# Running AV, MoE and w2*wout as pairs of 64-row tiles on TensorE, with scores in a ring of two

## The chip, the cores and the metric

The kernel runs on one core of one Trainium2 chip. Its engines work side by side, each through its own instruction stream in order, and meet at semaphores: TensorE (PE) multiplies matrices and writes to PSUM, ScalarE (ACT) and VectorE (DVE) read PSUM, GpSimd (POOL) casts inputs in SBUF, and SyncE (SP) issues nearly all transfers. PSUM has eight banks of 512 fp32 columns for each of 128 partitions. A matmul here is a weight load (the stationary operand, up to 128 rows by 128 columns) and a stream of up to 512 columns.

The metric is the device time in microseconds. Three timed runs of the kernel before gave 384.52, 386.2 and 386.59 us; their median is 386.2.

## The reference: what is computed

Attention with queries averaged in pairs, for batch 8, 8 heads, 1152 keys and head dimension 64, followed by an expert layer:

```python
q_pool = q.reshape(B, H, S // 2, 2, D).mean(axis=3)
scores = 1 / sqrt(D) * matmul(q_pool, k.transpose(0, 1, 3, 2))
attn   = softmax(scores)                       # over 1152 keys
x      = matmul(attn, v)   -> (4608 tokens, 512)
h1, h2 = x @ w1, x @ w2                        # 512 -> 1024
out    = maximum(h1, h2) @ w_out               # 1024 -> 512
```

The kernel uses max(h1, h2) = relu(x(w1 - w2)) + x w2. So it forms wd = w1 - w2 and w21 = w2*w_out once, computes g = relu(x wd), and then out = x w21 + g w_out.

## The kernel before, in words

**Stages.** The unit of attention is a pair of heads: 8 batches x 4 = 32 pairs. Q, K and V of a pair are loaded, cast to bf16 (queries are summed two by two) and transposed, the first pairs by TensorE, later ones by transposing transfers. The kinds of TensorE work are:

- *scores* (L429). The 9 key tiles x 576 queries of all pairs form one line, cut into 324 groups of 512 columns. Head dimension 64 fills half the array's rows, so the two heads of a pair use rows 0-63 and 64-127 as two tiles and write two banks. A group occupies one of three PSUM slots `sps` of two banks each.
- *exp* (L436). ScalarE reads one slot, 128x1024, and writes the exponentials as bf16 into `et`.
- *AV* (kind "a", L378). For one head: 5 chunks of queries, each a sum over 9 key tiles of a matmul with 128 rows and 65 columns (64 of V and one of ones, which gives the softmax's denominator). All chunks of a head go to one bank. VectorE takes the reciprocal (L388) and scales (L390).
- *x* (L489): after 4 pairs a batch's x is transposed; batches 0 and 7 by TensorE.
- *w* (L531, L547): w2 is transposed, then multiplied by w_out: 4 jobs of 8 matmuls.
- *h* (L582): for a block of up to 512 tokens, 8 jobs of 4 matmuls; VectorE applies relu into a ring of 1024 tokens (L593).
- *p* (L609): for 128 tokens, a job of 4 + 8 matmuls of 512 columns; the result is copied (L623) and stored (L567).

**How the order is made.** A planner in Python (class `Plan`) simulates the engines with costs and hand-over times (`LAT`), and emits instructions in the order in which it placed them. It also derives the semaphore waits, so on the chip each engine follows this fixed order. A `Job` is a list of units that accumulate into one bank, and an evacuation. Two `lane`s, one for each of the two banks `fb`, hold a job each. In each step (L906 to L937) free lanes are refilled in the order q, k, x, a, w, p, h; then a burst of two or three score groups is emitted if all of it can start now (`burst_now`, `burst_size`), otherwise the unit of highest rank (q, k, x, a, w, p, h) that is ready. Scores are emitted in bursts because the planner charges 0.1 us whenever TensorE goes between "s" (64 rows) and "f" (128 rows).

**The tail.** When all scores are out (`nxt == NGR`), the six banks of `sps` become six more lanes (`more_banks`), and ScalarE takes part in evacuations (L589, L620).

Of the kernel before, what the change touches and what calls it, by code (L numbers as in the profile page):

```python
# [7 lines left out]
P = 128  # L8
# [7 lines left out]
class Plan:  # L16
# [9 lines left out]
    LAT = {"PE": 0.16, "ACT": 0.13, "DVE": 0.1, "POOL": 0.05}  # L26
# [28 lines left out]
    def op(self, eng, fn, r=(), w=(), dma=None, cost=0.1, mode="f", after=(), solo=False):  # L55
        n = len(self.ops)
        assert all(k in self.writer for k in r), r
        deps, raw = self.deps(r, w, after)
        prev = self.last.get(eng)
# [4 lines left out]
        t = self.when(eng, r, w, after)  # L64
        if dma is not None:
# [9 lines left out]
        self.ops.append(dict(eng=eng, fn=fn, deps=deps, raw=raw, dma=dma, w=tuple(w),  # L75
                             seen=seen, end=self.free[eng], solo=solo))
# [7 lines left out]
    def solve(self):  # L84
# [3 lines left out]
        for n, o in enumerate(ops):  # L88
# [3 lines left out]
            for d in sorted(o["deps"], reverse=True):  # L92
                p = ops[d]
                if p["dma"] is None:
                    if p["eng"] == eng and (eng == "PE" or d not in o["raw"]):
# [50 lines left out]
class Job:  # L146


    def __init__(self, kind, units, evac, done=None, nb=None):
        self.kind, self.units, self.evac, self.done = kind, units, evac, done  # L150
        self.nb = nb


def bass_funnel_attn__then__act_maxout2_kernel(
# [12 lines left out]
    SQ = S // 2  # L167
# [16 lines left out]
    NGR = NPAIR * PW // W  # L184

    ctx = ExitStack()
    with ctx:
# [33 lines left out]
        sps = [psum([P, 2, 512], f"sps{g}") for g in range(3)]  # L221
        fb = [psum([P, 512], f"fb{g}") for g in range(2)]
        fb += [sps[g][:, half, :] for g in range(3) for half in range(2)]
# [84 lines left out]
        def unit(r, cost, go, mode="f"):  # L308

            def plan_it(m):  # L310
                op("PE", lambda e: go(e, m), r=r, w=[f"f{m}"], cost=cost, mode=mode)
            return r, plan_it, cost
# [52 lines left out]
        def av_jobs(i):  # L365
# [7 lines left out]
            def chunk(half, sb):  # L373

                def go(e, m):
                    for t in range(NT):
                        a = (half * 2 + es) * PW + t * SQ + sb * P
                        last = e.matmul(  # L378
                            fb[m][:, sb * 66:sb * 66 + 65], et[:, a:a + P],
                            vE[vs][:, t, half, 0:65], start=(t == 0), stop=(t == NT - 1))  # L380
                    return last
                return unit(need, 0.275, go)
# [14 lines left out]
            return [Job("a", [chunk(half, sb) for sb in range(NCH + 1)], norm(half), nb=i)  # L397
# [25 lines left out]
        def scores(g):  # L423
            r = g % 3
# [9 lines left out]
            def exp(a, z, keys):  # L434
# [3 lines left out]
                    r=[f"s{r}"], w=keys + [f"s{r}"], cost=0.24 + (z - a) / 700.0)  # L438
# [103 lines left out]
        def w21_jobs():  # L542
            jobs = []
            for ct in range(NC_):
                def part(ft, ct=ct):
                    def go(e, m):
                        return e.matmul(fb[m][:, :], w2T[:, ct, ft, :], wo[:, ft, :],  # L547
                                        start=(ft == 0), stop=(ft == NF - 1))
                    return unit([f"w2T{ct}", f"wo{ft}"], 0.216, go)
# [4 lines left out]
                jobs.append(Job("w", [part(ft) for ft in range(NF)], evac))  # L554
# [19 lines left out]
        def h_jobs(nb, tail):  # L574
# [4 lines left out]
            for ft in range(NF):  # L579
                def part(ct, ft=ft):  # L580
                    def go(e, m):
                        return e.matmul(fb[m][:, 0:size], wd[:, ct, ft * P:(ft + 1) * P],  # L582
                                        xT[:, ct, n0:n1], start=(ct == 0), stop=(ct == NC_ - 1))
                    return unit([f"wd{ct}"] + xkeys(n0, n1), 0.216 * size / 512, go)

                def evac(m, ft=ft):
                    w = [f"gT.{g}.{ft}" for g in gkeys(n0, n1)] + [f"f{m}"]
                    if tail and ft % 2:
# [7 lines left out]
                jobs.append(Job("h", [part(ct) for ct in range(NC_)], evac, nb=nb))  # L596
            return jobs

        def p_job(lo, tail):
            hi = lo + P  # L600

            def part(j):
                def go(e, m):
                    if j < NC_:
                        lhs, rhs = xT[:, j, lo:hi], w21[:, j, :]
                    else:
                        c = lo % RING
                        lhs, rhs = gT[:, j - NC_, c:c + P], wo[:, j - NC_, :]
                    return e.matmul(fb[m][:, :], lhs, rhs, start=(j == 0), stop=(j == NC_ + NF - 1))  # L609
                if j < NC_:  # L610
                    return unit([f"w21{j}"] + xkeys(lo, hi), 0.216, go)
                return unit([f"wo{j - NC_}", f"gT.{lo % RING // P}.{j - NC_}"], 0.216, go)

            def evac(m):
# [4 lines left out]
                if tail and ocount[0] % 2:  # L619
# [6 lines left out]
            return Job("p", [part(j) for j in range(NC_ + NF)], evac, nb=hi)  # L626
# [3 lines left out]
        lane = {0: None, 1: None}  # L630
# [23 lines left out]
        LAG = 600  # L654
        Q_PE = 5

# [100 lines left out]
        def more_banks():  # L757

            for g in range(3):
                for half in range(2):  # L760
                    m = 2 + 2 * g + half
                    lane[m] = None
                    plan.writer[f"f{m}"] = plan.writer[f"s{g}"]
                    plan.readers[f"f{m}"] = set(plan.readers[f"s{g}"])

        def ready_at(job):
            return plan.when("PE", r=job.units[0][0])

        def burst_size():

            done = [b for b in range(B) if all(av_half.get(b * NHP + j) == 2 for j in range(NHP))]
            return 3 if len(done) * SQ - p_end[0] > LAG else 2

        def more_moe():
            tail = nxt == NGR
            while h_at[0] < len(hblocks):
# [6 lines left out]
                queue["h"].extend(h_jobs(h_at[0], tail))  # L783
                h_at[0] += 1
            while p_at[0] + P <= h_end[0] and f"w21{NC_ - 1}" in plan.writer:
                queue["p"].append(p_job(p_at[0], tail))
                p_at[0] += P

        def refill():
# [3 lines left out]
            for kind in "qkxa":  # L793
                if queue[kind] and (ready_at(queue[kind][0]) <= soon):
                    return queue[kind].pop(0)
            busy = [j.kind for j in lane.values() if j]
            for kind in "wh" if queue["a"] and "p" in busy else "wph":
                if queue[kind] and ready_at(queue[kind][0]) <= soon:
                    return queue[kind].pop(0)
# [6 lines left out]
        def burst_now(size):  # L806

            todo_g = range(nxt, min(nxt + size, NGR))
            if not todo_g:
                return None, 0.0  # L810
            for g in todo_g:
                for p, t, *_ in pieces(g):
                    if p not in q_done or k_hi.get(p, 0) <= t or (
                            p >= 2 and av_half.get(p - 2) != 2):
                        return None, 0.0
            t = now() + 0.1
            stall = 0.0
            for g in todo_g:
                s = plan.when("PE", r=skeys(g), w=[f"s{g % 3}"])
                stall += max(0.0, s - t)  # L820
                t = max(t, s) + PE_S
            return todo_g, stall

        def emit_burst(todo_g):
            nonlocal nxt, entered
            for g in todo_g:
                while entered < pairs_of(g)[-1]:
                    entered += 1
                    enter(entered)
                scores(g)  # L830
                for p in pairs_of(g):
                    if g == after(p) - 1:
                        queue["a"].extend(av_jobs(p))
            nxt += len(todo_g)
            if nxt == NGR:
                more_banks()
            if queue["q"]:
                for kk in (0, 1):
                    if lane[kk] is None and plan.when(
                            "PE", r=queue["q"][0].units[0][0], w=[f"f{kk}"]) <= now() + 0.05:  # L840
                        lane[kk] = queue["q"].pop(0)
                        emit_unit(kk)
                        break

        def emit_unit(kk):
            job = lane[kk]
            plan_it = job.units.pop(0)[1]
            plan_it(kk)
            if job.units:
                return  # L850
            job.evac(kk)
            lane[kk] = None
            if job.kind == "a":
# [52 lines left out]
        while p_end[0] < NTOK:  # L906
            flush()
            for kk in sorted(lane, key=lambda kk: plan.when("PE", w=[f"f{kk}"])):
                if lane[kk] is None:
                    lane[kk] = refill()  # L910
            cand = []
            for kk in lane:
                job = lane[kk]
                if job is not None:
                    t = plan.when("PE", r=job.units[0][0], w=[f"f{kk}"])
                    cand.append((t, -rank[job.kind], len(job.units), kk))
            fresh = [c for c in cand if c[0] <= now() + 0.03]
            ready, stall = burst_now(burst_size())
            if ready and stall <= 0.1:
                emit_burst(ready)  # L920
            elif fresh:
                emit_unit(min(fresh, key=lambda c: c[1:])[3])
            else:
                wait = min([c[0] for c in cand], default=1e9) - now()
                if ready:
                    wait = min(wait, stall)
                size = burst_size()
                while size > 1 and (not ready or stall > 0.05):
                    size -= 1
# [63 lines left out]
```

## Time and profile before

| | |
|---|---|
| median of three timed runs | 386.2 us (384.52 to 386.59) |
| the profiled execution | 382.8 us, its span; the page gives no other time for it |
| PE busy | 363.7 us, 95% of the span |
| ACT busy | 316.9 us, 83% |
| DVE, POOL busy | 140.2 us (37%), 162.0 us (42%) |
| chain that ended last, by engine | PE 85%, DMA 6%, DVE 4%, POOL 2% |
| its largest lines | AV 22%, p 21% + 4%, scores 18%, h 15% + 2% |
| scores on TensorE | from 8.3 to 332.3 us |

How to read it: one execution, all times in us from its start unless marked ns. A row of a group has line, engine, operation, output<-inputs, rows*columns of the weights, shapes and count, then busy time and mean ns of one, then the engine's idle time before it and what ended that. A matmul's duration includes the time until its result is there, so matmuls that follow each other overlap and their starts tell the pace. In a timeline row the first number is the start, the second the time until the last of the merged instructions ended. A row of the chain has the start and the time that it stood in the chain.

### The profile page before, as it was taken

To read this page: it belongs to the slowest core of one execution; us is meant where nothing else is said; L and a number is where in the kernel's file an instruction comes from. 1 tells how busy PE (TensorE), PEld (TensorE's weight loads), DVE (VectorE), ACT (ScalarE), POOL (GpSimd) and SP (SyncE) were. 2 spreads that over 40 slices of the span, in tenths; PEclk is the share of its full clock that TensorE was granted. 3 is DMA by queue.
4 is the path that set the end of the run, shared out by engine and by line. 5 is a ranking of instruction groups with operands and counts; after the bars stand their busy time and mean duration, and the time that the engine had idled before them with its cause. 6 is when DMAs were issued, how large, how long until landed. Compare 5 with 4: busy or idle time off the path is not lost.

```text
span 382.8 us, 11318 instructions
## 1 busy us (share of the span) xinstructions
PE 363.7 (95%) x5010; PEld 210.8 (55%) x5010; DVE 140.2 (37%) x283; ACT 316.9 (83%) x355; POOL 162.0 (42%) x135
## 2 busy tenths in 40 slices
PE   2787999999999999999999999999999999999995
PEld 1365546555555555455556565555455655667642
DVE  2274934442234223422252224422442244237201
ACT  3998989999999999999999999999899999902210
POOL 1955597665554555555453535545545110000000
PEclk9999999999999999999999999999999999999999
DMA  8999999999989998999799999999899460121144
GB/s 248 405 391 399 392 257 312 331 309 312 225 234 295 273 272 174 309 320 275 142 265 289 319 179 212 286 258 315 200 236 267 94 109 14 29 44 42 29 95 98
DMA packets 93521, 88.58 MB, mean 231 GB/s; under 512 B 66080, under 2 KB 66592, under 8 KB 93472
## 3 DMA queue, kind: packets, MB, share of 16 engines
q1 hardware_dynamic: 93472, 87.86, 89.4%
q8 instruction: 39, 0.64, 0.7%
q14 instruction: 10, 0.08, 0.1%
HBM read 62.91 MB, written 9.44 MB: 189 GB/s over the span
## 4 chain that ended last, share of the span: by engine, by line
PE 85%; DMA 6%; DVE 4%; POOL 2%; issue 1%; SPq 1%; POOLq 0%
PE fb L378 22%; PE fb L609 21%; PE sps L429 18%; PE fb L582 15%; PE sps L609 4%; DMA qraw<-in_q_dram 3%; DMA kraw<-in_k_dram 2%; PE sps L582 2%; DVE wd L519 2%; POOL qp L297 1%; PE fb L547 1%; DVE xnat L390 1%; POOL vE L304 1%; PE fb L489 1%; DVE wo L523 1%
## 5 line engine op out<-in xcount | busy, mean ns | idle before, releaser
L436 ACT ACTIVATE et<-sps 128x1024 bf16<-128x1024 f32 (+1 forms) x336 | 307.8, 1005 | 19.0 <-PE sps L429 17.2
L378 PEld LDWEIGHTS fb<-vE,et 128*128 128x128 bf16 x2880 | 93.4, 97 | 20.9 <-issue 10.9
L378 PE MATMUL fb<-vE,et 128*128 128x65 bf16 x2880 | 101.9, 193 | 0.3
L297 POOL TENSOR_TENSOR qp<-qraw 64x576 bf16<-64x576 f32 x62 | 88.6, 1429 | 30.6 <-DMA qpT<-qp 21.3
L429 PE MATMUL sps<-qpT,kT 64*128 64x512 bf16 (+7 forms) x1152 | 96.9, 289 | 3.0 <-ACT et L436 2.1
L304 POOL TENSOR_SCALAR vE<-vraw 128x1152 bf16<-128x1152 f32 x32 | 36.9, 1152 | 103.2 <-PE fb L378 95.8
L429 PEld LDWEIGHTS sps<-qpT,kT 64*128 64x128 bf16 x1152 | 41.8, 95 | 51.3 <-issue 19.6
L582 PE MATMUL fb<-xT,wd 128*128 128x512 bf16 (+3 forms) x276 | 63.1, 360 | 0.7 <-DVE stage L623 0.7
L609 PE MATMUL fb<-wo,stage 128*128 128x512 bf16 x240 | 62.4, 380 | 0.0
L593 DVE TENSOR_SCALAR stage<-fb 128x512 bf16<-128x512 f32 (+3 forms) x64 | 41.9, 657 | 32.3 <-PE fb L582 32.1
L388 DVE RECIPROCAL rc<-fb 128x5 f32<-128x5 f32 x64 | 12.4, 194 | 112.3 <-PE fb L378 112.3
L273 POOL TENSOR_SCALAR kbf<-kraw 128x1152 bf16<-128x1152 f32 x31 | 36.2, 1167 | 14.6 <-DMA kraw<-in_k_dram 12.5
L582 PEld LDWEIGHTS fb<-xT,wd 128*128 128x128 bf16 x276 | 22.8, 98 | 29.4 <-DVE stage L593 6.3
L623 DVE COPY stage<-fb 128x512 f32<-128x512 f32 x29 | 20.0, 690 | 50.2 <-PE fb L609 49.7
L609 PEld LDWEIGHTS fb<-wo,stage 128*128 128x128 bf16 x240 | 21.1, 97 | 23.3 <-issue 3.3
L390 DVE TENSOR_TENSOR xnat<-fb,rc 128x320 bf16<-128x320 f32 x64 | 31.5, 491 | 2.2
L609 PE MATMUL fb<-w,xT 128*128 128x512 bf16 x120 | 32.1, 380 | 0.0
L609 PEld LDWEIGHTS fb<-w,xT 128*128 128x128 bf16 x120 | 10.3, 98 | 11.7 <-issue 2.0
L589 ACT ACTIVATE stage<-sps 128x256 bf16<-128x256 f32 (+1 forms) x7 | 2.3, 338 | 16.4 <-PE sps L582 16.4
L620 ACT COPY stage<-sps 128x512 f32<-128x512 f32 x3 | 1.8, 585 | 13.8 <-PE sps L609 13.8
L609 PE MATMUL sps<-wo,stage 128*128 128x512 bf16 x48 | 11.3, 379 | 0.0
L582 PE MATMUL sps<-xT,wd 128*128 128x256 bf16 (+2 forms) x76 | 10.3, 275 | 0.0
(40 smaller groups left out, 96.4 us busy)
## 6 DMA issues: line engine op xcount, KB each, us to landing
vraw<-in_v_dram SPq DMA_DIRECT2D x32, 576.0 KB, 7.7
kraw<-in_k_dram SPq DMA_DIRECT2D x31, 576.0 KB, 6.6
qraw<-in_q_dram SPq DMA_DIRECT2D x31, 576.0 KB, 5.8
out_dram<-stage SPq DMA_DIRECT2D x72, 128.0 KB, 2.4
xT<-in_moe_w_dram SPq DMA_DIRECT2D x4, 512.0 KB, 11.9
stage<-in_moe_w_out_dram SPq DMA_DIRECT2D x4, 512.0 KB, 14.2
stage<-in_moe_w_dram SPq DMA_DIRECT2D x4, 512.0 KB, 13.2
qraw<-in_q_dram SPq DMA_DIRECT2D x2, 288.0 KB, 4.1
```

The costliest lines, as they stand in the source:

```text
L273: op("POOL", lambda g: g.tensor_scalar(kbf[s][:, :, :, :].rearrange("p t h d -> p h t d"), kraw[r][:, :, :, :], 1.0, 1.0, ALU.mult, ALU.mu ...
L297: op("DVE" if i == 0 else "POOL", lambda g, half=half, a=a: g.tensor_tensor(qp[s][:, :, half, :], a[:, :, 0, :], a[:, :, 1, :], ALU.add), ...
L304: op("POOL", lambda g: g.tensor_scalar(vE[r][:, :, :, 0:D].rearrange("p t h d -> p h t d"), vraw[r][:, :, :, :], 1.0, 1.0, ALU.mult, ALU.m ...
L378: last = e.matmul(fb[m][:, sb * 66:sb * 66 + 65], et[:, a:a + P], vE[vs][:, t, half, 0:65], start=(t == 0), stop=(t == NT - 1))
L388: dve(lambda e: e.reciprocal(rc[half][:, :], a[:, :, 64:65]), [f"f{m}"], [f"rc{half}"], 0.19)
L390: dve(lambda e: e.tensor_tensor(xnat[xs][:, :, c:c + D], a[:, :, 0:D], rc[half][:, :].unsqueeze(2).to_broadcast([P, NCH + 1, D]), ALU.mult ...
L429: last = e.matmul(sps[r][:, h, col:col + hi - lo], kT[i % 3][rows(h), t, :], qpT[i % 3][rows(h), lo:hi], start=True, stop=True)
L436: op("ACT", lambda e: e.activation(et2[:, :, c:c + z - a], sps[r][:, :, a - g * W:z - g * W], EXP, scale=scale), r=[f"s{r}"], w=keys + [f" ...
L582: return e.matmul(fb[m][:, 0:size], wd[:, ct, ft * P:(ft + 1) * P], xT[:, ct, n0:n1], start=(ct == 0), stop=(ct == NC_ - 1))
L593: dve(lambda e: e.tensor_scalar_max(gT[:, ft, g0:g0 + size], fb[m][:, 0:size], 0.0), [f"f{m}"], w, 0.1 + size / 960.0)
L609: return e.matmul(fb[m][:, :], lhs, rhs, start=(j == 0), stop=(j == NC_ + NF - 1))
L623: dve(lambda e: e.tensor_copy(osb[o][:, :], fb[m][:, :]), [f"f{m}"], [f"osb{o}", f"f{m}"], 0.63)
```

## The change

**Pairs.** AV, h, p and w2*wout jobs are marked `split`. Before the last score, two neighbouring jobs of the same kind are taken together as a `Pair`, in a lane of two banks. Each matmul of 128 rows becomes two of 64 rows. In the first half the lower rows work on job one and the upper rows on job two, each into its own job's bank; in the second half the lower rows work on job two and the upper rows on job one. So each job gets both halves of its rows in turn, and the two tiles never write the same bank at the same time. Before the first unit of the second half TensorE waits on its own semaphore until the last matmul of the first half is complete (`gate`); the planner holds that unit back for another 0.2 us (`GATE`), during which it may place other units. When the pair ends, both banks are evacuated one after the other. Only the first matmul of a bank has `start` set. Paired units have mode "s", like the scores.

**Scores.** `sps` becomes a ring of two (`NS = 2`); the banks that this frees give two lanes of two banks. Groups are emitted one at a time, as soon as the slot is free, if the array is in mode "s", or ScalarE would soon run out, or no unit of mode "f" is ready. The bursts go.

**Planner.** The hand-over of ScalarE is now 0.2 us (0.13 before), and an exponential costs 0.08 + columns/612 (0.24 + columns/700 before): 0.917 us for a whole group instead of 0.971. Units of the current mode come first when that mode is "f".

**Tail.** When all scores are out, lanes that are free are split into lanes of one bank (`part_lanes`), and jobs run singly with 128 rows as before.

```diff
-    LAT = {"PE": 0.16, "ACT": 0.13, "DVE": 0.1, "POOL": 0.05}
+    LAT = {"PE": 0.16, "ACT": 0.2, "DVE": 0.1, "POOL": 0.05}
...
+class Pair:
+    def __init__(self, one, two):
+        self.kind, self.jobs = one.kind, (one, two)
+        self.units = []
+        n = len(one.units)
+        for phase in range(2):
+            for k, (u, v) in enumerate(zip(one.units, two.units)):
+                low, high = (u, v) if phase == 0 else (v, u)
+                parts = []
+                for j, (p, q) in enumerate(zip(low.parts, high.parts)):
+                    first = phase == 0 and k == 0 and j == 0
+                    last = phase == 1 and k == n - 1 and j == len(u.parts) - 1
+                    parts.append((p, q, phase, first, last))
+                r = list(dict.fromkeys(list(u.r) + list(v.r)))
+                self.units.append(Unit(r, u.cost * 1.01, "s", parts=parts, gate=phase == 1 and k == 0))
...
-        sps = [psum([P, 2, 512], f"sps{g}") for g in range(3)]
-        fb = [psum([P, 512], f"fb{g}") for g in range(2)]
+        sps = [psum([P, 2, 512], f"sps{g}") for g in range(NS)]
+        S0 = 8 - 2 * NS
+        fb = [psum([P, 512], f"fb{g}") for g in range(S0)]
...
+            def crossed(e):
+                for p, q, phase, first, fin in u.parts:
+                    for half, (at, lhs, rhs, *_), m in ((0, p, ms[phase]), (1, q, ms[1 - phase])):
+                        last = e.matmul(fb[m][:, at:at + rhs.shape[-1]], lhs[rows(half)], rhs[rows(half)],
+                                        start=first, stop=fin)
+                return last
...
-            r = g % 3
+            r = g % NS
...
-                    r=[f"s{r}"], w=keys + [f"s{r}"], cost=0.24 + (z - a) / 700.0)
+                    r=[f"s{r}"], w=keys + [f"s{r}"], cost=0.08 + (z - a) / 612.0)
...
+        def part_lanes():
+            for kk in range(S0 // 2):
+                if lane[kk] is None and len(at_bank[kk]) == 2:
+                    one, two = at_bank[kk]
+                    at_bank[kk] = (one,)
+                    lane[S0 + two] = None
+                    at_bank[S0 + two] = (two,)
...
+        def lane_at(kk):
+            u = lane[kk].units[0]
+            t = plan.when("PE", r=u.r, w=fk(banks_for(kk, lane[kk])))
+            return max(t, plan.ops[gates[kk]]["seen"] + GATE) if u.gate else t
...
+        def take(kind, by):
+            line_up = queue[kind]
+            if not line_up:
+                return None
+            if nxt == NGR or not line_up[0].split:
+                if ready_at(line_up[0]) <= by:
+                    return line_up.pop(0)
+            elif len(line_up) > 1 and line_up[1].split and max(ready_at(j) for j in line_up[:2]) <= by:
+                return Pair(line_up.pop(0), line_up.pop(0))
+            return None
...
-            ready, stall = burst_now(burst_size())
-            if ready and stall <= 0.1:
-                emit_burst(ready)
+            same = [c for c in fresh if lane[c[3]].units[0].mode == plan.mode]
+            ts = score_at()
+            starving = plan.free.get("ACT", 0.0) < now() + 0.6
+            if ts is not None and ts <= now() + 0.03 and (plan.mode != "f" or starving or not same):
+                emit_scores()
             elif fresh:
-                emit_unit(min(fresh, key=lambda c: c[1:])[3])
+                emit_unit(min(same if plan.mode == "f" and same else fresh, key=lambda c: c[1:])[3])
```

More of the change, by code (lines that the diff above doesn't have):

```diff
@@ L373, in chunk @@
             def chunk(half, sb):
[L375 to L382, printed above, removed]
+                parts = []
+                for t in range(NT):
+                    a = (half * 2 + es) * PW + t * SQ + sb * P
+                    parts.append((sb * 66, et[:, a:a + P], vE[vs][:, t, half, 0:65], t == 0, t == NT - 1))
+                return mm_unit(need, 0.275, parts)
             def norm(half):
@@ L553, in evac @@
                         [f"f{m}"], [f"w21{ct}", f"f{m}"], 0.63)
[L554 removed]
+                jobs.append(Job("w", [part(ft) for ft in range(NF)], evac, split=True))
             return jobs
```

204 lines of the change are left out of this document (100 added, 104 removed).

## The prediction

> **What bounds the kernel now.** I read the page first, then the groups by shape, then the chain of waits and the timeline around single bursts of scores. The page says who is busy:
>
> ```profile
> span 382.8 us, 11318 instructions
> PE 363.7 (95%) x5010; PEld 210.8 (55%) x5010; DVE 140.2 (37%) x283; ACT 316.9 (83%) x355; POOL 162.0 (42%) x135
> PE   2787999999999999999999999999999999999995
> ACT  3998989999999999999999999999899999902210
> ```
>
> TensorE is at nine tenths or more in 35 of 40 slices. ScalarE, which does the exponentials, is nearly as full, but stops at about slice 35. A stretch from the middle of the chain of waits shows that nothing but TensorE work stands in it:
>
> ```profile
> 107.81 0.76 PE sps L429 x12
> 108.57 1.40 PE fb L582 x6
> 109.97 1.18 PE fb L378 x36
> 111.15 0.76 PE sps L429 x12
> 111.91 1.74 PE fb L378 x54
> ...
> 117.41 0.76 PE sps L429 x12
> 118.17 2.36 PE fb L582 x10
> ...
> 123.53 0.05 issue
> ```
>
> So what ends the kernel is the sum of what TensorE must do, plus the time in which it is busy in name only. The latter shows where the kind of work changes. Scores (L429) use two tiles of 64 rows; everything else here uses all 128:
>
> ```profile
> 107.21 0.59 PE L582 MATMUL fb<-xT,wd 128*128 128x512 bf16 x2
> 107.74 0.83 PE L429 MATMUL sps<-qpT,kT 64*128 64x128 bf16 x12
> 108.50 0.39 PE L582 MATMUL fb<-xT,wd 128*128 128x512 bf16 x1
> ...
> 363.14 15.55 PE sps L609 x72
> ```
>
> In the last row 72 matmuls of 512 columns take 15.55 us, 0.216 each. The two that start at 107.21 should therefore release the array at 107.64; the scores start at 107.74, 0.10 later. The twelve score matmuls are three groups of 512 columns, two heads at a time: 3 x 0.216 = 0.65, so 108.39; the next work starts at 108.50, 0.11 later, of which about 0.02 lies inside the six pairs. A change between 64 and 128 rows costs about 0.095 us each way.
>
> **The change, part by part.**
>
> *Changes of row mode.* I counted them down TensorE's rows of the timeline: 261 neighbours differ in rows. The first and the last:
>
> ```profile
> 6.72 0.66 PE L323 MATMUL fb<-ident,qp 64*128 64x64 bf16 x9 [6.72 <-DVE qp L297]
> 7.31 0.50 PE L349 MATMUL fb<-ident,kbf 128*128 128x128 bf16 x3
> 346.52 0.29 PE L489 MATMUL sps<-ident,xnat 64*128 64x64 bf16 x4
> 346.74 0.34 PE L582 MATMUL sps<-xT,wd 128*128 128x384 bf16 x1
> ```
>
> 261 x 0.095 = 24.8 us. After the change AV, h, p and w2*wout are 64-row work like the scores. What stays at 128 rows before the last score is the transposes of K (10 jobs), of w2 (4) and of batch 0 (4), each with two changes at most, 36, and the return to 128 rows for the tail, about 4. 221 fall away: **-21.0 us**. If transposes bunch, only 10 stay (-23.8); if pairs and transposes alternate badly, 60 (-19.1).
>
> *Two tiles in place of one.* Each old matmul becomes two of half the rows, and two jobs run side by side, so the array's time is unchanged only if tiles truly overlap. For 512 columns the scores settle it: three groups in 0.65 us are the full rate. AV with its 65 columns is the harder case:
>
> ```profile
> L378 PE MATMUL fb<-vE,et 128*128 128x65 bf16 x2880 | 101.9, 193 | 0.3
> 154.00 1.53 PE L378 MATMUL fb<-vE,et 128*128 128x65 bf16 x45
> 61.28 0.20 PE L429 MATMUL sps<-qpT,kT 64*128 64x64 bf16 x1
> 61.30 0.19 PE L489 MATMUL fb<-ident,xnat 64*128 64x64 bf16 x1
> 61.32 0.35 PE L429 MATMUL sps<-qpT,kT 64*128 64x448 bf16 x1
> 61.33 0.19 PE L489 MATMUL fb<-ident,xnat 64*128 64x64 bf16 x1
> 61.36 0.38 PE L429 MATMUL sps<-qpT,kT 64*128 64x64 bf16 x2
> 153.32 0.11 PEld L429 LDWEIGHTS sps<-qpT,kT 64*128 64x128 bf16 x4 [0.24 <-ACT et L436]
> ```
>
> 45 AV matmuls take 1.53 less the 0.19 of one, so 30 ns each. Two tiles that overlap need a pair per 30 ns. Around 61.3 two lines happen to run on different tiles: five matmuls start within 0.08 us, 20 ns apart, and those of L489 keep their 30 ns from 61.30 to 61.33 while L429 starts one between. At 153.32 four weight loads together take 0.11 us, where one takes 0.095: they start within 0.02. Bounds: 0 if tiles overlap fully; if every AV matmul kept today's 30 ns to itself, 2880 x 0.030 = +86 us. The rows lie near the first. I take **+1 us**, for a few ns between the two starts.
>
> The Trainium skill (TensorE: Matmul & The Clock Gate, section "Wait — 56ns, not 53.3ns?") speaks against this edit: start-to-start never falls below about 25 ns however narrow a matmul is. The 20 ns row says that the floor does not hold across tiles, but it is a short row; I keep the rule as a rival.
>
> *The swap halfway.* Each pair waits once, on TensorE's own semaphore, for the last matmul of its first half (a gate). Rows for its price:
>
> ```profile
> L378 PE MATMUL fb<-vE,et x2880: 190/192/205, 19.9 to 339.2; 128*128 128x65 bf16 x192
> L582 PE MATMUL fb<-xT,wd 128*128 128x512 bf16 (+1 forms) x232 | 57.9, 379 | 0.7 <-DVE stage L623 0.7
> L609 PE MATMUL fb<-wo,stage 128*128 128x512 bf16 x200 | 52.4, 380 | 0.0
> L609 PE MATMUL fb<-w,xT 128*128 128x512 bf16 x100 | 26.9, 380 | 0.0
> L547 PE MATMUL fb<-wo,xT 128*128 128x512 bf16 x32 | 8.3, 381 | 0.8 <-DVE w L552 0.8
> ```
>
> A matmul's result is there 0.19 us (AV) or 0.38 us (512 columns) after its start, where the stream would have gone on after 0.03 or 0.22; a hand-over to TensorE shows as 0.05 ("issue" at 123.53). An uncovered gate costs 0.16 + 0.05 = 0.21 us, and as TensorE runs its queue in order, everything queued behind it, scores too, waits along, and then ScalarE. Pairs: 2880/90 = 32 of AV; about 232/8 = 29 of h and (200 + 100)/24 = 12 of p, by the counts between 60 and 330 us; 32/16 = 2 of w2*wout: 75. All uncovered: 16 us. What hides it is a unit of the other lane, or a score group, put between; the planner may do that (it holds a gated unit back by 0.2 us more). Cover fails while the other lane's banks are being emptied. I take a third, **+5 us**, with 0 and 16 as ends.
>
> *Emptying two banks at once.* A pair ends with both evacuations in a row on VectorE:
>
> ```profile
> L593 DVE TENSOR_SCALAR stage<-fb 128x512 bf16<-128x512 f32 x56 | 38.7, 691 | 30.6 <-PE fb L582 30.4
> L388 DVE RECIPROCAL rc<-fb 128x5 f32<-128x5 f32 x64 | 12.4, 194 | 112.3 <-PE fb L378 112.3
> L390 DVE TENSOR_TENSOR xnat<-fb,rc 128x320 bf16<-128x320 f32 x64 | 31.5, 491 | 2.2
> ```
>
> The lane is then shut for 2 x 0.69 = 1.4 us instead of 0.7, twice as long for twice the work, and the other lane covers it as now: matmuls of L582 sat idle for a VectorE evacuation 0.7 us in all. Without cover 0.7 us more per pair would be 52 us; with it 0. I take **+1 us** and 5 as the upper end.
>
> *Scores singly, in a ring of two.* ScalarE's rows:
>
> ```profile
> 300.61 4.69 ACT L436 ACTIVATE et<-sps 128x1024 bf16<-128x1024 f32 x5 [0.18 <-PE sps L429]
> 305.46 4.75 ACT L436 ACTIVATE et<-sps 128x1024 bf16<-128x1024 f32 x5 [0.17 <-PE sps L429]
> L436 ACT ACTIVATE et<-sps 128x1024 bf16<-128x1024 f32 x312 | 295.4, 1035 | 18.0 <-PE sps L429 16.6
> ```
>
> One takes 1.035 us, but back to back they start (4.69 - 1.03)/4 = 0.915 apart. A slot's round is 1.035, a hand-over of 0.05, at most one unit in TensorE's way (nine pairs of AV, 0.28) and 0.22 for the scores: 1.59, under 2 x 0.915 = 1.83. So a ring of two can feed ScalarE without a gap, if no gate or evacuation wait stands in front of the scores. Its 18 us of idle may shrink; that is off the end, since TensorE sums up the work: 0.
>
> *The tail.* After the last score 46 us of 128-row work remain, of which the scheme changes nothing; part of it (p and h of finished batches) moves ahead of the last score as the earlier stretch gets room. Not counted twice: 0.
>
> **Sum.** -21 + 1 + 5 + 1 = -14 on the span of 382.8 us, so 368.8. The page gives no other time for the profiled execution; the timed runs lie 1.7 to 3.8 us above its span and their median, 386.2, 3.4 above. The same 3.4 on top: **372 us**.
>
> **The rivals.**
>
> *B, the gates and bank pairs eat the gain.* All 75 gates uncovered (16 us) and evacuations at their upper end (5): -21 + 1 + 16 + 5 = +1, so 387. For it: 29 of the pairs are of h, whose halves last only 4 x 0.216 = 0.87 us while the other lane's banks need 1.4. Against: AV and p are long, and scores come every 0.915 us as filler.
>
> *C, the ring of two starves ScalarE: slower.* The answer for the line of the scores gives the span of the scores:
>
> ```profile
> L429 PE MATMUL sps<-qpT,kT x1152: 189/296/606, 8.3 to 332.3; 64*128 64x512 bf16 x24, 64*128 64x128 bf16 x24, 64*128 64x320 bf16 x24, 64*128 64x448 bf16 x24
> ```
>
> Today 324 groups (32 pairs x 9 x 576 columns / 512) start from 8.3 to 332.3 us, 1.0 us apart, and the last is followed by 50 us. Of these about 27 can't be moved ahead: AV of the last pair (90 x 0.030 = 2.7), its transposes (about 1), h of 576 tokens (32 x 576 columns at 0.216 per 512, 7.8), p (4.5 x 12 x 0.216, 11.7) and some 4 us after TensorE's end. If each group comes s apart, the time is 8.3 + 324 s + 27 + 3.4, which passes 386.2 at s = 1.07: a slot's round of 2.14, so 0.8 us of other work or waiting before each group in place of 0.28. With one gate and two units ahead of each group s would be about 1.1, and the time 395. For it: bursts of three hid such delays, and a ring of two has only 0.24 us to spare. Against: the changed planner issues a group as soon as its slot is free and puts ScalarE's cadence at 0.917.
>
> *D, narrow matmuls don't overlap.* By the 30 ns bound the time is 372 + 85 = 457; the decision is whether 61.3's rows hold for 90 pairs in a row.
>
> By the 25 ns of the Trainium skill (TensorE: Matmul & The Clock Gate, the same section) a pair would take 50 ns in place of 30, +58 us, an estimate of 430 us; it is the milder form of D.
>
> *E, the rows are not the cost:* were the 0.095 us something that follows scores anyway (a wait for a slot), removing the mode change would gain nothing: 386 + 7 = 393. It shows the same both ways, and where no semaphore comes in between, so I give it no more than a remainder, counted with D.
>
> **How the numbers follow.** Forecast 0.74, B 0.12, C 0.08, D with E 0.06. The forecast's own range, from the ends of its terms, is 382.8 + 3.4 - 23.8 = 362 to 386.2 - 19.1 + 2 + 8 = 377 (half of the gates uncovered). The range for 8 in 10 is stretched down by some us for early gaps that close and up through most of B: 360 to 388. A measurement of this kernel tells about 0.5% from no change: faster means under 384.3, slower over 388.1. The forecast is nearly all faster; B spreads, a third each way and to no change; C, D and E are slower: faster 0.78, same 0.04, slower 0.18.
>
> **What the changed profile would show.** Changes of row mode down to some 40, and L429 next to 64-row L378, L582 and L609 without the 0.10. AV rows of 64 rows, 18 in about 0.28 us; 0.5 would be D. Waits of TensorE on itself near 5 us; 15 would be B. ScalarE's idle time under 18 us; above 40, C. The last score near 315 to 325 us with a tail shorter than 46. I am wrong if the time is above 377 or below 362, or right by accident if TensorE's stream grows and its waits shrink.

## The result, and the profile after

The changed kernel takes 430.73 us (median of four runs, 428.13 to 433.87), the kernel before, run beside it, 385.78 us: a ratio of 1.119, 95% interval 1.112 to 1.125. 372 was forecast, with 388 as the upper end. The kernel became 45 us slower. The times below leave out a few runs that the chip did in a slower state, such as 1236 us where the others took 444 to 447.

The page of the changed kernel, with the same rows as before, and with the granted clock and the queue that brings instructions:

```profile
span 426.4 us, 18068 instructions
PE 364.5 (85%) x8389; PEld 229.2 (54%) x8392; DVE 137.9 (32%) x277; ACT 316.7 (74%) x361; POOL 164.9 (39%) x135
PE   3787869977978798969978898979779989999996
ACT  4878777986898687977788768978589969922211
PEclk9999898998999899997999999999899999999999
q8 instruction: 66, 1.08, 1.1%
PE 66%; ACT 20%; issue 9%; DVE 2%; DMA 1%; SPq 1%; POOL 0%
```

TensorE's busy time is the same (364.5 against 363.7 us) in a span that is 43.6 us longer: it stands in holes that it didn't have. ScalarE thins out in the same way. In the chain of waits 9% is now "issue" (1% before), time in which an engine waits for nothing that the profile shows. TensorE has 8389 matmuls and 8392 weight loads (three records of matmuls are missing) where it had 5010 of each.

The waits of the changed kernel (engine, output and line, what it waited for: us in total, times, longest):

```profile
ACT et L488 <- PE sps L481: 60.7, 42, 4.0
PE fb L360 <- issue: 34.9, 22, 4.1
PE sps L481 <- ACT et L488: 10.4, 22, 0.7
PEld fb L360 <- PE fb L360: 6.4, 13, 0.6
PEld fb L360 <- DVE stage L641: 3.6, 9, 0.5
```

The fourth is the gates, the fifth the emptying of banks. The second is new. What answered to the first, the third and the second in the kernel before:

```profile
ACT et L436 <- PE sps L429: 17.2, 57, 1.0
PE sps L429 <- ACT et L436: 2.1, 5, 0.5
PE fb L531 <- issue: 0.3, 1, 0.3
```

The timeline of TensorE, and after the line of "..." that of ScalarE, around one of the 22 "issue" waits:

```profile
186.64 0.72 PE L360 MATMUL fb<-vE,et 64*128 64x65 bf16 x36
187.40 0.40 PE L481 MATMUL sps<-qpT,kT 64*128 64x320 bf16 x4
187.62 0.63 PE L360 MATMUL fb<-vE,et 64*128 64x65 bf16 x30
192.22 0.35 PE L360 MATMUL fb<-vE,et 64*128 64x65 bf16 x6 [3.97 <-issue]
192.36 0.64 PE L481 MATMUL sps<-qpT,kT 64*128 64x384 bf16 x4
...
184.26 4.83 ACT L488 ACTIVATE et<-sps 128x1024 bf16<-128x1024 f32 x5
193.03 1.02 ACT L488 ACTIVATE et<-sps 128x1024 bf16<-128x1024 f32 x1 [3.94 <-PE sps L481]
```

TensorE stops in the middle of a unit of AV, which in a pair has 18 matmuls: 30 of 36 are done, the other six come 4 us later. They read the same `et` and `vE` and write the same banks, so no data, bank or score slot can hold them. ScalarE, whose next scores stand behind them, stops as well. The first row also gives the pace: 36 matmuls in 0.72 - 0.19 = 0.53 us, 15 ns each. The two tiles do overlap, a pair per 30 ns.

**What the stalls have in common.** The trace records each instruction of TensorE and each packet of the instruction queue. 1.08 MB in 66 packets is 16 KB each; with two instructions per matmul, some 16,780 in all, a packet is 256 of them. Seven of the 22 stalls over 0.6 us, by count of instructions:

```
instruction  its number  gap     packet      next
             mod 256     ns      landed us   instruction us
   961       193         1755     37.22       38.72
  1985       193         4329     62.34       63.89
  3521       193         2512     96.81       98.17
  5569       193         2441    145.22      146.50
  7617       193         4160    190.89      192.22
 11713       193         2642    283.00      284.40
 14785       193         1537    348.69      350.16
```

All 22 stand at number 193 of a block of 256, and each ends 1.3 to 1.6 us after a packet has landed. They sum up to 41 us from start to start; the waits show 34.9 of it at L360 (2.5 more at L481), as a wait begins only when the matmul before it has ended. The other gaps over 0.6 us, between 20 us and the last matmul, are all in front of scores and stand at other numbers. **TensorE has run out of instructions.** Near the end, where no loads are under way, a packet starts some 280 instructions before its first one is needed (265 to 285 in the last four), so it seems to be asked for about one block ahead. With loads under way it starts later; how much later is counted from that place. From records of the same kind:

```
                                   before    after
instructions of TensorE            10,020    some 16,780
time per 256, median us            9.0       5.8
time per 256, shortest us          6.1       2.8
packet starts late by, median us   3.1       3.4
  the latest us                    6.3       8.1
transfer of a packet us            1.05      1.03
```

Before, 256 instructions last 6.1 us at least and 9.0 in the middle, longer than the 3.1 + 1.05 + 1.4 = 5.6 us of a middling packet; the latest packets left little room, and the closest one landed 1.4 us before its first instruction ran. Pairs of AV at 15 ns per matmul, two instructions each, would use up a block in 2 us, by that pace. The Trainium skill (Runtime: NRT & Kernel Launch, "Instruction fetch mechanics") says that instructions come in blocks of 16 KiB, 256 of them, which the trace bears out, and that the fetch is mostly hidden; here it is not.

**The other losses.** Windows of the changed kernel around the stall (columns: length, busy us (count) of PE, PEld, DVE, ACT, POOL, granted clock, DMA share, GB/s):

```profile
188.10:192.20 4.10, 0.15 (x10) 0.04 (x3) 0.00 (x0) 1.00 (x2) 0.00 (x0) 0.88 1.27 122
191.20:198.00 6.80, 5.78 (x84) 3.45 (x85) 2.57 (x6) 3.39 (x4) 3.35 (x3) 0.50 1.00 359
198.00:205.00 7.00, 7.00 (x81) 3.84 (x78) 0.44 (x1) 6.87 (x8) 1.71 (x2) 1.00 1.13 260
```

The clock is at half from 191.2 to 198.0, mostly after TensorE has resumed. There are six such stretches of 3.4 or 6.8 us, and none in the kernel before. Five begin within 1.1 us of the end of a stall of 2.4 to 4.3 us, the sixth among three gaps of 0.8 to 0.9 us; one stall of 2.6 us, at 284, has none behind it. The mean clock says what they cost at most:

```profile
core 0: 426.4 us, clock 0.972
```

0.028 x 426 = 12 us. So the 43.6 us are about: changes of row mode, now 35 in place of 261, -226 x 0.095 = -21.5; missing instructions +41; half clock +12; TensorE waiting for a score slot +8 (10.4 - 2.1); gates +6.4. That is +46, some of it counted twice, since stalls and half clock overlap.

### The profile page after: what moved, and what is told of

Its sections match the earlier page's. It is cut to its first block, busy times and chain, and to the rows that moved or that the text cites. A ratio compares the mean times of both kernels' runs of the same rounds, so it can differ in the third digit from the quotient of the medians.

```text
span 426.4 us, 18068 instructions
## 1 busy us (share of the span) xinstructions
PE 364.5 (85%) x8389; PEld 229.2 (54%) x8392; DVE 137.9 (32%) x277; ACT 316.7 (74%) x361; POOL 164.9 (39%) x135
## 3 DMA queue, kind: packets, MB, share of 16 engines
q8 instruction: 66, 1.08, 1.1%
## 4 chain that ended last, share of the span: by engine, by line
PE 66%; ACT 20%; issue 9%; DVE 2%; DMA 1%; SPq 1%; POOL 0%
PE fb L360 43%; ACT et L488 20%; PE sps L481 13%; PE fb L354 5%; PE sps L354 4%; DMA kraw<-in_k_dram 1%; DVE stage L641 1%; PE fb L405 1%; PE fb L541 0%; SPq L291 0%; POOL kbf L306 0%; SPq L280 0%; DVE xnat L442 0%; PE fb L379 0%; DVE stage L669 0%
## 5 line engine op out<-in xcount | busy, mean ns | idle before, releaser
L488 ACT ACTIVATE et<-sps 128x1024 bf16<-128x1024 f32 (+1 forms) x336 | 304.6, 1027 | 61.6 <-PE sps L481 60.7
L360 PE MATMUL fb<-vE,et 64*128 64x65 bf16 x5580 | 115.9, 193 | 34.6 <-issue 34.5
L481 PE MATMUL sps<-qpT,kT 64*128 64x512 bf16 (+7 forms) x1152 | 131.0, 297 | 14.2 <-ACT et L488 10.4
L360 PEld LDWEIGHTS fb<-vE,et 64*128 64x128 bf16 x5580 | 106.9, 96 | 52.2 <-issue 38.1
L481 PEld LDWEIGHTS sps<-qpT,kT 64*128 64x128 bf16 x1152 | 47.9, 96 | 66.7 <-ACT et L488 44.7
L360 PE MATMUL fb<-xT,wd 64*128 64x512 bf16 x448 | 66.3, 383 | 0.7 <-DVE xnat L442 0.2
L360 PE MATMUL fb<-wo,stage 64*128 64x512 bf16 x448 | 63.6, 376 | 0.0
L360 PE MATMUL fb<-w,xT 64*128 64x512 bf16 x224 | 35.8, 398 | 0.8 <-issue 0.4
L360 PEld LDWEIGHTS fb<-wo,stage 64*128 64x128 bf16 x448 | 23.1, 94 | 14.6 <-issue 0.2
L360 PEld LDWEIGHTS fb<-xT,wd 64*128 64x128 bf16 x448 | 20.3, 95 | 17.5 <-PE fb L360 3.1
L360 PEld LDWEIGHTS fb<-w,xT 64*128 64x128 bf16 x224 | 11.6, 100 | 11.8 <-PE fb L360 3.3
L360 PE MATMUL fb<-wo,xT 64*128 64x512 bf16 x64 | 10.3, 417 | 0.0
L354 PE MATMUL fb<-wo,stage 128*128 128x512 bf16 x40 | 9.4, 379 | 0.0
```

The source lines that it names most:

```text
L354: last = e.matmul(fb[ms[0]][:, at:at + rhs.shape[-1]], lhs, rhs, start=start, stop=stop)
L360: last = e.matmul(fb[m][:, at:at + rhs.shape[-1]], lhs[rows(half)], rhs[rows(half)], start=first, stop=fin)
L481: last = e.matmul(sps[r][:, h, col:col + hi - lo], kT[i % 3][rows(h), t, :], qpT[i % 3][rows(h), lo:hi], start=True, stop=True)
L488: op("ACT", lambda e: e.activation(et2[:, :, c:c + z - a], sps[r][:, :, a - g * W:z - g * W], EXP, scale=scale), r=[f"s{r}"], w=keys + [f" ...
```

## The experiments

Theory F: TensorE's instructions arrive late, because their packets queue behind the loads and the pairs use them up fast. Against it: S (R in the expectations), the ring of two or single scores starve the engines; N, a floor per matmul that holds across tiles; G, the figures of the planner; and for what remains, the pairs themselves. The times of the kernel before beside these runs were 384.0 to 384.4 us.

**Loads nearly without bytes.** In the changed kernel and in the one before, the order being the same:

```diff
-                kraw[s][:, :, lo:hi, :],
+                kraw[s][0:P if i < 3 else 1, :, lo:hi, :],
```

and alike for Q and V and their sources.

> The changed kernel with every load of Q, K and V from the fourth pair on cut to one partition (its bytes left out, so old data are used; the order of all engines' instructions, the waits and the transposing transfers stay). Theory F (TensorE's instructions arrive late: a block of 256 is asked for only when the block before it begins, and its 16 KB packet queues behind the loads): the packets start earlier, TensorE's 22 stalls of together 41 us fall below 15 us, the half-clock stretches after them go, and the time falls from 431 to 385-400 us. What may stay is a residue of some 0.4 us per dense block, since 256 AV instructions last about 2.1 us and a packet 1.05 plus the 1.4 us from its landing to the next instruction. Theory R (the ring of two and single scores starve ScalarE): no change, 425-435. Theory N (a floor per matmul in TensorE that holds across tiles): no change, 425-435.

393.81 us, ratio 1.025 (1.022 to 1.028). Its span, clock and waits:

```profile
core 0: 391.3 us, clock 0.995
PE fb L364 <- issue: 10.3, 13, 1.6
PE sps L485 <- ACT et L492: 11.3, 25, 0.7
PEld fb L364 <- PE fb L364: 6.6, 14, 0.6
```

The same instructions in the same order are 37 us faster when the loads are gone. Stalls over 0.6 us go from 22 to 9, together from 41 to 11 us, the late start of a packet from 3.4 to 1.6 us. F holds, and N falls, as the matmuls are the same. Waits for a slot and gates stay.

> The kernel before with the same loads cut to one partition (bytes left out). The control of the run on the changed kernel: theory F expects at most 1% less than 386, since no block of 256 instructions is late there; if transfers themselves bound the kernel before, over 3% less.

386.74 us, ratio 1.006 (1.005 to 1.008). The kernel before gains nothing from it, so the 37 us are not what loads cost this work in general.

**Which part brings the stalls.** First AV alone is left whole, then all kinds:

```diff
-            return [Job("a", [...], norm(half), nb=i, split=True)
+            return [Job("a", [...], norm(half), nb=i)
```

> The changed kernel with AV alone left in 128 rows, one job at a time (5562 matmuls in place of 8392, 317 changes of row mode in place of 35); h, p and w2*wout stay paired, scores stay single in a ring of two. Theory F: no late blocks (under 3 us of such stalls), 282 x 0.095 = 27 us of mode changes come back, 41 + 12 us of stalls and half clock go: 388-402 us. Theory R: ScalarE is starved as before, 425 or more plus the 27 us. Theory N: AV's floor goes as well, so the time is like F's; N and F are told apart by the run with tiny loads.

393.06 us, 1.022 (1.020 to 1.025). Its span, its matmuls and a wait:

```profile
core 0: 391.1 us, clock 0.986
PE 373.1 (95%) x5562; PEld 218.6 (56%) x5562; DVE 137.2 (35%) x276; ACT 318.4 (81%) x362; POOL 163.1 (42%) x135
PE sps L481 <- ACT et L488: 5.2, 12, 0.9
```

No packet stops TensorE, although packets start as late as before the edit (3.3 us in the middle): the shortest block of 256 now lasts 6.2 us. The pairs of AV, which double the densest stream of instructions, bring the 22 stalls.

```diff
-            if nxt == NGR or not line_up[0].split:
+            if True:
```

> The changed kernel with no pairs at all: single jobs of 128 rows, scores one by one in a ring of two, two lanes (5010 matmuls, 607 changes of row mode). Theory F: no late blocks; against the kernel before 346 more changes of mode, 33 us, and a few us for the ring: 415-430 us. Theory R: the ring itself costs 40 us or more, so 455 or more.

419.84 us, 1.093 (1.090 to 1.096). Without pairs nearly every single score group changes the row mode twice: 607 changes, 346 more than before, 33 us by 0.095, and the time is 36 us above. Its waits:

```profile
PE sps L481 <- ACT et L488: 3.8, 11, 0.7
ACT et L488 <- PE sps L481: 7.3, 10, 1.1
PE fb L354 <- issue: 1.0, 1, 1.0
```

A ring of two costs TensorE 1.7 us more than the ring of three, and ScalarE waits less for scores than in the kernel before (7.3 us, 17.2 there). The ring and the single scores by themselves are not the cause; beside pairs the waits for a slot are larger, 11.3 us with loads away. The wait on "issue" is a late packet too, at number 193 and 1.4 us behind a landing: one, where none was expected.

**Stalls without pairs.** The kernel before, with AV's 65 columns cut in two, so that there are 2880 more matmuls of 128 rows, two tiles nowhere but in the scores:

```diff
-                    for t in range(NT):
+                    for lo, hi in ((0, 33), (33, 65)):
+                        for t in range(NT):
...
```

> The kernel before, with each AV matmul of 65 columns cut into one of 33 and one of 32 columns, with the same weights loaded again (7890 matmuls in place of 5010; all 128 rows, no pairs, bursts, a ring of three; the result is unchanged). Theory F: late blocks appear here too, at the same place in every block of 256 instructions as in the changed kernel, 5 to 20 of them, and on top the AV stream grows if a matmul of 33 columns takes over 15 ns: 390-470 us. If the late blocks belong to row tiles or to the ring of two, none appears.

464.6 us, a single run. A row of its waits, and one of its timeline:

```profile
PE fb L379 <- issue: 16.5, 9, 3.1
202.97 2.43 PE L379 MATMUL fb<-vE,et 128*128 128x33 bf16 x90
```

Nine packets are late by the same sign, 18 us in all, in a kernel without the change; counted by weight loads, as 54 records of matmuls are missing, all nine stalls stand at number 193. (Most of the other time is the work itself: 90 matmuls in 2.43 - 0.19 us are 25 ns each, so a halved matmul costs 25 in place of 30.) F again.

**The planner's figures.** The kernel before with ScalarE's hand-over of 0.2 and an exponential of 0.08 + columns/612:

> The kernel before with only the change's two planner figures (ScalarE's hand-over 0.2 in place of 0.13 us, an exponential 0.08 + columns/612 in place of 0.24 + columns/700), and the wait of the last AV chunk on the exponentials beside its own columns, without which this order would read them unsynchronised (259 changes of row mode, before 261; bursts, ring of three, no pairs). Theory F gives the figures no part in the loss: 382-388 us. If the new figures are what places scores wrongly in the changed kernel, over 390.

384.82 us, 1.0015 (1.0002 to 1.0028): by themselves the figures cost nothing. The changed kernel with the old figures was not tried.

**Spreading the instructions out.** After a unit of AV, two units of the other lane come first:

```diff
+                         key=lambda c: (lane[c[3]].kind == "a" and since[0] < APART, *c[1:]))[3]
+                since[0] = 0 if lane[kk].kind == "a" else since[0] + 1
```

> The changed kernel with one rule more in the planner's choice: after a unit of AV the next two units are taken from the other lane, if it has one ready (8376 matmuls, 31 changes of row mode, the same work). So a block of 256 instructions holds AV and 512-column matmuls mixed and lasts longer. Theory F: fewer and shorter late blocks (41 us fall to 10-25), but not none, because a packet needs in the middle 3.4 us of queueing, 1.05 of transfer and 1.4 more, which is near the 5.6 us that an average block then lasts: 400-418 us. Theory R: no change, 425-435. Theory N: no change.

447.01 us, 1.159 (1.154 to 1.164): a miss. Its span and clock, and its waits:

```profile
core 0: 445.3 us, clock 0.935
PE fb L360 <- issue: 25.7, 17, 4.5
PE sps L481 <- ACT et L488: 23.3, 45, 0.9
```

Late blocks fall from 41 to 33 us, where 10 to 25 were expected, but waits for slots grow by 13 us and the loss to half clock to 0.065 x 445 = 29 us.

**Fewer loads at a time.** Each load waits until the load two before it has landed, then the one before it:

```diff
+                before = [loaded[x] for x in list(loaded)[-2:-2+1 or None]]
...
+                plan.ops[-1]["deps"].update(before)
```

In the second run both 2s are 1s.

> The changed kernel with the same order on every engine; each load issued in the loop waits on SP until the load two before it has landed, so at most two loads stand in the queues at a time. Theory F: the instruction packets queue less (3.4 us in the middle now, 1.6 with tiny loads), late blocks fall from 41 us to 15-32, 405-425 us, if the loads themselves still come in time. If the packets' delay has nothing to do with loads that are queued ahead, 428-433 or more.

459.08 us, 1.193 (1.190 to 1.196). The rows of its waits:

```profile
PE fb L360 <- issue: 22.9, 15, 3.5
PE fb L360 <- DMA xT<-xnat: 21.5, 5, 5.8
```

> As the run with two loads, but each load waits until the one before has landed. Theory F: late blocks fall further, under 25 us, but three loads a pair of some 1.5 us and two us of latency each take about 10.5 us, more than the 9.3 us that ScalarE needs for a pair, so POOL and then TensorE wait for transfers: 400-430 us.

570.12 us, 1.491 (1.482 to 1.500). The same rows:

```profile
PE fb L360 <- issue: 9.4, 10, 2.3
PE fb L360 <- DMA xT<-xnat: 77.1, 6, 16.2
```

With the queue shorter, the late blocks shrink as F says, from 41 to 29 to 10 us. This shows less than the run without bytes, because TensorE also stood for data here and so used up its instructions more slowly. The times missed by far: waiting loads hold up the transposing transfers behind them on SyncE, and the data come late.

**A better kernel from the part that works?** AV whole, all else in pairs, and AV left for scores only when ScalarE has been out of work for 0.3 us:

```diff
-            starving = plan.free.get("ACT", 0.0) < now() + 0.6
+            starving = plan.free.get("ACT", 0.0) < now() - 0.3
```

and in the second run 0.3 us before it is out, `now() + 0.3`. (A last chunk of AV reads 64 columns beyond its own, and in these two runs waits for what writes them; so does the run with the planner's figures.)

> AV whole in 128 rows and single, the rest paired, as before, and now the planner leaves a run of AV units for a score group only when ScalarE has been out of work for 0.3 us, instead of 0.6 us before it runs out; the last AV chunk waits also for the exponentials whose columns it reads beside its own (159 changes of row mode, 5618 matmuls). Theory F with 0.095 us for each change: 158 changes fewer than with the first rule, 15 us, so 374-384 us, and no late block; ScalarE idles more, which costs nothing as long as the last score comes before 335 us. If single scores in a ring of two bound it instead, the time stays at 390 or grows.

407.01 us, 1.058 (1.055 to 1.061): a miss. Row mode changes only 159 times, but a wait and the windows show what came of it:

```profile
PE sps L481 <- ACT et L488: 19.3, 41, 0.7
103.00:106.80 3.80, 1.64 (x16) 0.50 (x16) 0.19 (x1) 3.80 (x6) 3.63 (x4) 1.00 0.96 343
106.80:113.60 6.80, 6.15 (x83) 4.18 (x84) 0.69 (x2) 4.30 (x5) 0.94 (x1) 0.50 1.08 180
113.60:120.00 6.40, 5.85 (x84) 3.42 (x83) 1.97 (x4) 5.63 (x7) 5.01 (x4) 1.00 0.97 214
```

After runs of AV only scores are left; TensorE does 1.64 us of work in 3.80 and waits for slots, and then the clock is halved for 6.8 us. No packet is late in this run, so half clock doesn't need one. The Trainium skill (TensorE: Matmul & The Clock Gate, "What's actually happening") has the clock at half after an idle window of some 3.4 us, in windows of 3413 ns. The lengths agree, once or twice 3.4 us; the idle window does not show here, as TensorE was busy 43% of the 3.80 us and no matmul waited over 0.53 us.

> AV whole in 128 rows and the rest paired, with the planner leaving a run of AV units for scores when ScalarE is within 0.3 us of running out (247 changes of row mode; the two runs of this kind so far had 317 and 159). If the loss of the run with 159 comes from TensorE running out of work between batches, then idling and falling to half clock, this one lies between: 70 x 0.095 = 6.6 us less than the 393 of the first, less whatever idles, so 386-394 us, with fewer than two stretches of half clock after the first 50 us. If score waits in the ring of two bound it, 393-407 in proportion to the changes removed.

395.97 us, 1.030 (1.028 to 1.032), with 247 changes: above the 386 to 394 of the first account, and within the 393 to 407 of waits for slots.

```profile
PE sps L481 <- ACT et L488: 11.8, 24, 0.9
```

With the 0.6 us of the run in which AV alone was whole there were 317 changes, 5.2 us of such waits and 393.06 us. The 70 changes saved, 6.7 us by 0.095, are given back as 6.6 us more of waits for a slot. None of these kernels beats the one before.

## Why the prediction was wrong

**The step that failed is "Two tiles in place of one", +1 us.** As the prediction put it, "the array's time is unchanged only if tiles truly overlap", and the bounds were whether they do. They do: 15 ns between the starts. But the step priced the array alone; the bringing of instructions has no term in the sum, which put it at nothing without a reason. Halving the rows doubles the instructions of AV, and these have to be brought at twice the pace. The row on which it leaned, five matmuls around 61.3 us, shows what TensorE does with a handful of instructions already at hand; it can say nothing of 90 pairs in a row, and the prediction asked only whether the overlap would hold so long, not the supply. Behind this one term stand 41 us of stalls and most of the 12 us of half clock: with loads away 11 and 2 us of them are left.

**The other terms.** *Changes of row mode*: -21.0 forecast, -21.5 by the count of 226 fewer, at 0.095 as before. That they are gone shows in the rows, too; here scores and p of the changed kernel follow each other while both still run:

```profile
105.32 0.38 PE L481 MATMUL sps<-qpT,kT 64*128 64x128 bf16 x4
105.53 0.81 PE L360 MATMUL fb<-w,xT 64*128 64x512 bf16 x6
```

The p work starts 0.21 us after four score matmuls, the time that their two pairs stream; no 0.10 lies between. With nothing paired, 346 more changes went with 36 us, 0.10 each. So E falls. *Gates*: +5 forecast, 6.4 in 13 waits of weight loads; behind all 74 gates together the matmuls start 6.0 us later than their stream would have them. *Two banks emptied at once*: +1 forecast; the weight loads' waits for it are 3.6 us in 9, and no wait of a matmul is put down to it; it is not what cost the time. *Scores in a ring of two*: 0 forecast, +8 measured, the second term that was mis-sized. The reckoning, 1.59 against 1.83 us, let at most one unit stand before a score group; where TensorE has just stood still, ScalarE has run dry and TensorE waits for it afterwards. But with loads away and few stalls, 11.3 us of it remained, so it is no echo of the stalls alone; with nothing paired it was 3.8. How much is due to gated units in front of the scores was not told apart. With loads away the terms are -21.5 + 11 of stalls + 2 of half clock + 9 of slots + 6.6 of gates = +7, against 8.5 us in the span.

**The rivals.** B falls: gates 6.4 of 16 us. C has its sign, ScalarE idle above 40 us, 60.7 in fact, but not its cause: a ring of two with nothing paired leaves ScalarE idle for 7.3 us, and the rise of its idle time, 44 us over the 17.2 before, is about the 41 us in which TensorE had no instructions; with loads away it is 27.7. D falls as a mechanism. The estimate by the Trainium skill (TensorE: Matmul & The Clock Gate, "Wait — 56ns, not 53.3ns?") came out at 430, where the time is, by accident: its 25 ns between starts do hold inside one tile, as the halved AV of 128 rows shows, and do not hold across two, at 15 ns. Of the signs named for the forecast, mode changes near 40, 18 matmuls in 0.28 us and waits on itself near 5 came; ScalarE idle under 18 us, the last score at 315 to 325 and a tail under 46 us did not. The last score came at 373, with 53 us behind it:

```profile
L481 PE MATMUL sps<-qpT,kT x1152: 187/296/631, 8.1 to 373.2; 64*128 64x128 bf16 x25, 64*128 64x64 bf16 x25, 64*128 64x512 bf16 x24, 64*128 64x320 bf16 x24
```

Without any late packet the change would still have gained little: taking the 10.3 us of stalls that remained from the 391.3 us with loads away leaves 381, an estimate, against 382.8 before.

**Open.** Why a packet of instructions starts up to 8 us late is not settled: fewer loads shorten it (3.4 us; 3.1 and 1.9 with loads held back; 1.6 with loads nearly empty), which speaks for a queue behind them. The changed kernel's own trace says the same: of its packets, the 11 for which the data queue filled less than half of the DMA engines' time in the 2 us around the place where they are due start 1.1 us late in the middle, the others 3.8. But no run changed the packets' place among the loads.

## What to carry to other kernels

Before matmuls are halved to run on two tiles, count the instructions: 256 of TensorE's must last longer than it takes to bring the next 256, here about 3.4 + 1.05 + 1.4 = 6 us under heavy loads and 1.6 + 1.05 + 1.4 = 4 us with loads nearly empty, both estimates from middling packets; the latest here took 8.1 in place of the 3.4. A short dense burst in a trace shows instructions already at hand and prices nothing that lasts. And price what a saved cost will expose: here waits for score slots took back a part of each change of mode that was removed, and a stretch in which TensorE stands still or has little to do can be paid a second time at half clock, as behind five stalls of 2.4 to 4.3 us here.

## What was not expected of the hardware

An engine can stop for want of instructions in a stream without branches: 22 times, up to 4.3 us from start to start, always at number 193 of a block of 256, and the profile calls it only "issue". Two 64-row tiles pass a matmul of 65 columns every 15 ns, where one 128-row tile needs 30 for 65 columns and 25 for 33 or 32. And on a single core the granted clock falls to 0.50 for 3.4 or 6.8 us behind stalls of 2.4 to 4.3 us, and in another run behind 3.8 us in which TensorE was 43% busy and no packet was late.
